# Score items in pairs, key scores together, two heads in one transposing DMA, packed steps reordered

## The chip, the cores and the metric

One core of a Trainium2 chip runs the whole kernel. The metric is the device time of one execution in microseconds. In the profile PE is the matrix engine (TensorE) and PEld its weight loads, DVE is VectorE, ACT is ScalarE, POOL is GpSimd, and SP issues the DMAs.

## The reference, cut to what matters

Three stages run behind each other for 8 batches of 576 tokens.

```
# 1 packed attention, 8 heads of 64, 32 packed rows p per head
p_packed = softmax(p k^T / 8) v              # "key scores" s, then a, pp
out      = softmax(q p_packed^T / 8) p_packed # "second scores", a2
# 2 gated MLP on x = out (576 x 512)
u, v   = split(gelu(x @ w_in));  v_n = layernorm(v) * g_ln
v_s    = w_sg @ v_n + b_sg;      x = x + (u * v_s) @ w_out
# 3 four causal attention experts of width 64, top 2 of 4 per token
for e in range(4):
    a   = softmax(causal((x wq_e)(x wk_e)^T / 8))
    out += weight_e * (a (x wv_e)) wo_e
```

## The kernel before, in words

The kernel goes through the batches in a software pipeline. A turn of the loop consists of `front(b)` and `back(b)`. `front` forms the v half of the gated MLP (`v_tiles`) and its u half (`u_tile`, four tiles). `back` forms v_s (`vs_tile`, four tiles), then the q and k products of the experts (`qk`, groups 0 to 3; the first part from gh, the second from a2 and bdq), their values and gate logits (`vlog`, token groups VT[0] to VT[2]) and the gates. The weights w_out are folded into the expert weights, and the packed rows of the next batch are folded into w_in, w_qk and w_vg (`wprime`, `bdw`: blocks wp, bdq, bdv).

The experts' attention is cut into ten items i = (j, pr): j is a group of 128 query tokens (j = 4 has 64), and pr is a pair of experts (0 for even i, 1 for odd i). S_i are the scores with their softmax (`att`: a product with 64 rows for each of the two experts; `att_last` for j = 4, S8 and S9, with a full-height padded copy `last_q`). T_i transposes the weights `at` into PSUM (block aTp), and ACT copies them out (aT). y_j multiplies with the values, ACT copies the result and DVE forms its remainder; o_j multiplies with w_o and ACT copies the result to ot. The last items of a batch run in the turn of the next one, and go(names) issues them.

The packed attention of the next batch runs in steps between the qk and vlog products of `back`. Q is one of two groups of four heads: K and Q join the planes of k and q on POOL (kT, qT), s is the key score with its exponential a, a (step) transposes it (a1T, DVE copies to a1t), p is the product with v (pp), P transposes that (ppT), r the second scores. Before that, SP turns k and q by a DMA (`turn`: DMA transpose; `keep`: write to DRAM; `planes`: read back). The list TURN holds those steps, and tick() issues the next of them.

PE and SP follow the program order (manual_schedule). The order on DVE, ACT and POOL is set by a scheduler. All PSUM blocks share one ring, pd, of four buffers, and each block of PE's work takes the next one.

In one batch turn of before, the row-split score items S1, S3, S5, S4 and S6 stand singly between the vs tiles and behind them, and S7, S0, S2 between qk and wp products. Key scores s0 and s1 are apart, with the exponential of one over other products.

Of the kernel before, what the change touches and what calls it, by code (L numbers as in the profile page):

```python
# [7 lines left out]
F32 = mybir.dt.float32  # L8
# [3 lines left out]
U16 = mybir.dt.uint16  # L12
# [5 lines left out]
P = 128  # L18
# [8 lines left out]
def packed_attention_mlp_moe_kernel(  # L27
# [18 lines left out]
    nc = tc.nc  # L46
    B, H, S, D = q.shape
# [10 lines left out]
    sb = ctx.enter_context(tc.tile_pool(name="sb", bufs=1))  # L58
# [1 line left out]
    psum = ctx.enter_context(tc.tile_pool(name="psum", bufs=1, space=bass.MemoryType.PSUM))  # L60
    dram = ctx.enter_context(tc.tile_pool(name="dram", bufs=1, space=bass.MemoryType.DRAM))

    NB = {"A": 4, "B": 10, "C": 4, "D": 12, "a": 3, "p": 1, "T": 4, "nat": 2, "x": 2, "t": 4, "v2": 1, "y": 1, "W": 2}
    NPS = 4
    BY = {"A": 1152, "B": 576, "C": 640, "D": 576, "a": 1152, "p": 576, "T": 512, "t": 576, "W": 2048}

    def slot(tag, dt=F32, w=None, name=None):
        t = sb.tile([P, BY[tag]], dt, tag=tag, name=name or ("s" + tag), bufs=NB[tag])
        return t if w is None else t[:, :w]
# [8 lines left out]
    def dap(src, offset, ap):  # L78
        return bass.AP(tensor=src.tensor, offset=src.offset + offset, ap=ap)
# [87 lines left out]
    def load_w_sg(c):  # L167
        if c < 4:
            if c % 2 == 0:
                wst["t"] = slot("A", name="wst")  # L170
            wst[c] = wst["t"][:, (c % 2) * S:(c % 2) * S + S]
        else:
            wst[c] = slot("p", name="wst")
        nc.sync.dma_start(wst[c][:TOK[c]], moe_w_sg[c * P:c * P + TOK[c], :])


# [148 lines left out]
    def load_nat(name, src, b, j):  # L325
        if (b, name) == (0, "q"):
            t = slot("T", w=512, name=name)
        elif (b, name) == (0, "v"):
            if j % 2 == 0:
                NAT["v2"] = slot("A", name=name)  # L330
            t = NAT["v2"][:, (j % 2) * 512:(j % 2) * 512 + 512]
        elif (b, name) == (0, "k") and j >= 2:
            t = slot("D", w=512, name=name)
        else:
            t = nat_slot(F32, name)
        t = t.rearrange("p (h n) -> p h n", h=2)
        off = (b * H + 2 * j) * S * D
        NAT[name, b, j] = t
        if b:
            for h in range(2):  # L340
                nc.sync.dma_start(t[:, h].rearrange("p (c d) -> p c d", c=4),
                                  dap(src, off + h * S * D, [[D, P], [P * D, 4], [1, D]]))
            if j % 2 == 0:
                r = small.tile([P, 2, D], F32, tag="rem", name=name + "r", bufs=2)
                for h in range(2):
                    nc.sync.dma_start(r[:, h], dap(src, off + (512 + 32 * h) * D, [[S * D, 4], [D, 32], [1, D]]))
                NAT[name + "r", b, j // 2] = r.rearrange("p h d -> p (h d)")
            return
        nc.sync.dma_start(t, dap(src, off, [[4 * D, P], [S * D, 2], [1, 4 * D]]))
        if j % 2 == 0:  # L350
            if name == "v":
                r = small.tile([P, 2 * D], F32, tag="rem", name=name + "r", bufs=2)
            else:
                if "rem" not in NAT:
                    NAT["rem"] = sb.tile([P, 512], F32, tag="y", name="rem", bufs=NB["y"])
                i = 2 * "kq".index(name) + j // 2
                r = NAT["rem"][:, i * P:(i + 1) * P]
            nc.sync.dma_start(r, dap(src, off + 512 * D, [[S * D, 4], [2 * D, 32], [1, 2 * D]]))
            NAT[name + "r", b, j // 2] = r
# [6 lines left out]
    def tick(n=1):  # L366
        for _ in range(min(n, len(TURN))):
            for f in TURN.pop(0):
                f()

    def p1_steps(b):
# [12 lines left out]
        def load(name, src, j):  # L384
            load_nat(name, src, b, j)
# [6 lines left out]
            act_copy(pT, pt[:, :2 * P], scale=0.125)  # L392
            s["pT"] = pT

        def turn(name, src, h):
            x = sb.tile([P, S], U16, tag="x", name=name + "x", bufs=NB["x"])
            nc.sync.dma_start_transpose(x, src[b, h].bitcast(U16))
            if h % 2 == 0:
                s[name + "x", h // 2] = dram.tile([P, 2, S], U16, name=f"turned_{name}{b}{h}")
            s["x", name, h] = x  # L400

        def keep(name, h):
            nc.sync.dma_start(s[name + "x", h // 2][:, h % 2, :], s.pop(("x", name, h)))
# [154 lines left out]

        last = None
        for name, src in (("k", k), ("q", q)):  # L560
            for h in range(H):
                TURN.append([lambda a=last: a and keep(*a), lambda a=(name, src, h): turn(*a)])
                last = (name, h)
        TURN.append([lambda a=last: keep(*a)])

        def f_():
            for j in range(4):
                planes("k", j)
            for j in range(2):
# [148 lines left out]
    def u_tile(b, m):  # L718
        s = ST[b]
        u = slot("D", name="u")  # L720
        pt = pd("u")
        n = 0
        for x, y in PASSES:
            for Q in range(2):
                for h in range(2):
                    nc.tensor.matmul(pt[:, h, :HALF], wp_part(b, 0, y, Q)[:, m * P:(m + 1) * P],  # L726
                                     s["a2", Q][x][:, hs(h)], start=n == 0, stop=n == 5)
                n += 1
        nc.scalar.activation(two(u), pt[:, :, :HALF], AF.Gelu_apprx_tanh)
        s["u", m] = u  # L730
# [308 lines left out]
    def front(b, go):  # L1039

        for cs in VT:
            v_tiles(b, cs)
            tick(2)
        u_tile(b, 0)
        go("T0")
        tick()
        for m in range(1, 4):
            u_tile(b, m)
            tick()

    def back(b, go):
        def do_all(names):

            for n in names.split():
                if (b + 1, n) in STEP:
                    STEP.pop((b + 1, n))()
                elif n[0] in "STyo":
                    go(n)

        if b:  # L1060
            go("S1")
            vs_tile(b, 0)
            go("S3")
            vs_tile(b, 1)
            go("T1 y0 T2 S5")
            vs_tile(b, 2)
            go("T3 o0 S4 y1")
            vs_tile(b, 3)
        tick(len(TURN))
        if b + 1 < B:  # L1070
            STEP.pop((b + 1, "f"))()
        go("T5 S6 o1 T4")
        bdw(b)
        weights(b + 1, ("in1", "in0"))
        nxt = attention(b)
        qk_mm(b, 0)
        go("S7 y2")
        qk_out(b, 0)
        do_all("K0 S8 T6 o2 s0 S9 T7")
        keep_last_q(b, 0)  # L1080
        qk(b, 2)
        if b + 1 == B:
            go("y3 T8 o3")
            vlog(b, VT[2])
            go("T9")
            vlog(b, VT[0])
            go("y4")
        else:
            do_all("y3 a0 K1 s1 Q0 p0 T8 o3 a1 T9 Q1")
            vlog(b, VT[2])  # L1090
            do_all("y4 p1 P0 o4 P1 r0 r1")
            if b + 2 < B:
                ahead(b + 2)
            vlog(b, VT[0])
            tick()
# [12 lines left out]
        tick()
        if b + 1 < B:
            wp_mm(b + 1, 1)  # L1110
        qk_gated(b, 3, False)
        tick()
        if b + 1 == B:
            qk_out(b, 3)
            return nxt
        wp_out(b + 1, 1)
        qk_out(b, 3)
        wprime(b + 1, 0)
        weights(b + 1, ("qk", "vg"))
# [144 lines left out]
```

## Time and profile before

| | |
|---|---|
| median of three runs | 879.46 us (879.15 to 879.69) |
| profiled execution, its own time | 878.9 us |
| its span | 877.0 us |
| mean granted clock of TensorE | 0.981 |
| PE busy | 825.4 us (94%) |
| DVE busy | 583.3 us (67%) |
| ACT busy | 424.7 us (48%) |
| POOL busy | 188.4 us (21%) |

The span is the time from the first to the last instruction of the profiled execution; the time of the execution is 1.9 us more. Busy times are sums over all instructions of an engine, and engines run beside one another.

### The profile page before, as it was taken

Reading aid. Unit: us, or ns where it says so; the run is one execution under the profiler, and the core shown is the slowest. Engines: PE = TensorE matmul, PEld = TensorE weight load, DVE = VectorE, ACT = ScalarE, POOL = GpSimd, SP = SyncE. Lnnn points to the kernel's source line nnn. Section 1 sums busy time; section 2 is a strip of 40 time slices with the busy share of each in tenths; the row PEclk is TensorE's granted clock in tenths of the full one; section 3 lists DMA queues with packets and bytes.
Section 4 is the critical chain, followed back from the end, with each engine's and each line's share of the span. In section 5 each row is a group of like instructions: output and inputs, shape, how many; then the busy total and the mean of one; then the engine's idle time right before and its main releaser. Section 6 shows DMA issues by size and latency. Waiting matters only on the chain.

```text
span 877.0 us, 19165 instructions
## 1 busy us (share of the span) xinstructions
PE 825.4 (94%) x7517; PEld 697.9 (80%) x7517; DVE 583.3 (67%) x1387; ACT 424.7 (48%) x973; POOL 188.4 (21%) x272
## 2 busy tenths in 40 slices
PE   4687988999999999999999999999999999999987
PEld 2356877788888888888789888888789888888965
DVE  6766644876577674877477665867488566866265
ACT  2356332565436542655346552655346543745245
POOL 0002051312332151303322141404222141300000
PEclk9798889999999999999999999999999999999989
DMA  9886673537445563548245563549263660100001
GB/s 307 229 208 176 143 234 86 146 88 224 114 99 143 140 188 86 154 109 231 76 130 116 148 188 83 154 111 237 69 153 89 171 178 7 74 13 26 19 1 55
DMA packets 178725, 114.08 MB, mean 130 GB/s; under 512 B 118282, under 2 KB 166666, under 8 KB 175820
## 3 DMA queue, kind: packets, MB, share of 16 engines
q1 hardware_dynamic: 178636, 112.87, 48.0%
q8 instruction: 59, 0.97, 0.5%
q14 instruction: 30, 0.25, 0.1%
HBM read 68.26 MB, written 29.63 MB: 112 GB/s over the span
## 4 chain that ended last, share of the span: by engine, by line
PE 75%; DVE 5%; ACT 2%; issue 1%; POOL 0%; ACTq 0%; DVEq 0%; POOLq 0%
PE vs L744 10%; PE qk L789 10%; PE y L968 6%; PE vlog L832 6%; PE qk L801 5%; PE v L676 5%; PE o L999 5%; PE sc L885 4%; PE u L726 4%; PE aTp L939 4%; PE vlog L836 3%; PE sc L915 2%; PE wp L625 1%; PE aTp L953 1%; PE s L448 1%
## 5 line engine op out<-in xcount | busy, mean ns | idle before, releaser
L744 PE MATMUL vs<-w_sg,vnh 128*128 128x288 f32 x512 | 92.8, 304 | 0.7 <-DVE w_sg L85 0.7
L789 PE MATMUL qk<-gh,w_qk 128*128 128x288 f32 x512 | 92.7, 304 | 0.0
L789 PEld LDWEIGHTS qk<-gh,w_qk 128*128 128x128 f32 x512 | 76.2, 193 | 10.6 <-issue 7.1
L82 ACT ACTIVATE aT<-aTp 128x512 f32<-128x512 f32 (+4 forms) x160 | 60.9, 434 | 44.1 <-PE aTp L939 36.2
L744 PEld LDWEIGHTS vs<-w_sg,vnh 128*128 128x128 f32 x512 | 75.7, 191 | 5.3 <-issue 3.0
L416 POOL COPY kT<-kp 128x576 uint16<-128x576 uint16 x56 | 48.0, 921 | 147.4 <-DMA kp<-turned_k 98.1
L898 ACT ACTIVATE at<-sc,nm 128x256 f32<-128x256 f32 (+3 forms) x128 | 66.3, 524 | 26.7 <-DVE nm L889 21.1
L691 POOL TENSOR_TENSOR rstd<-rstd,mhalf 128x1 f32<-128x1 f32 x40 | 36.4, 917 | 152.8 <-DVE rstd L690 152.8
L968 PE MATMUL y<-aT,v 128*64 128x128 f32 (+2 forms) x960 | 61.6, 267 | 0.2 <-ACT aT L82 0.2
L902 DVE TENSOR_SCALAR at<-at,sm,gw 128x256 f32<-128x256 f32 (+3 forms) x128 | 60.1, 511 | 2.3
L832 PE MATMUL vlog<-w_vg,gh 128*128 128x260 f32 (+1 forms) x320 | 60.8, 287 | 0.0
L968 PEld LDWEIGHTS y<-aT,v 128*64 128x64 f32 (+1 forms) x960 | 48.4, 140 | 14.1 <-issue 7.6
L819 POOL CAST last_q<-qk 64x64 fp32r<-64x64 f32 x64 | 14.9, 233 | 196.6 <-ACT qk L809 103.1
L789 PE MATMUL qk<-gl,w_qk 128*128 128x288 f32 x256 | 55.6, 299 | 0.0
L744 PE MATMUL vs<-w_sg,vnl 128*128 128x288 f32 x256 | 55.3, 298 | 0.0
L889 DVE TENSOR_REDUCE nm<-sc 128x2 f32<-128x256 f32 (+3 forms) x64 | 52.6, 822 | 1.7
L999 PE MATMUL o<-w_o,y 128*128 128x512 f32 x192 | 52.5, 408 | 0.5 <-ACT y L978 0.5
L832 PEld LDWEIGHTS vlog<-w_vg,gh 128*128 128x128 f32 (+1 forms) x320 | 47.4, 178 | 3.5 <-issue 2.8
L885 PE MATMUL sc<-qk 64*128 64x256 f32 (+3 forms) x384 | 47.4, 352 | 0.0
L416 POOL COPY qT<-qp 128x576 uint16<-128x576 uint16 x56 | 44.6, 870 | 11.0 <-DMA qp<-turned_q 11.0
L939 PE MATMUL aTp<-ident,at 128*128 128x128 f32 x320 | 46.6, 277 | 0.0
L899 DVE TENSOR_SCALAR sm<-sm 128x2 f32<-128x2 f32 x64 | 16.4, 256 | 44.9 <-ACT at L898 44.5
(208 smaller groups left out, 1927.9 us busy)
## 6 DMA issues: line engine op xcount, KB each, us to landing
w_in<-kept_in SPq DMA_DIRECT2D x14, 1024.0 KB
w_qk<-kept_qk SPq DMA_DIRECT2D x8, 1024.0 KB
out_dram<-ot SPq DMA_DIRECT2D x32, 256.0 KB
turned_k<-kx SPq DMA_DIRECT2D x56, 144.0 KB
turned_q<-qx SPq DMA_DIRECT2D x56, 144.0 KB
kp<-turned_k SPq DMA_DIRECT2D x56, 144.0 KB
qp<-turned_q SPq DMA_DIRECT2D x56, 144.0 KB
v<-in_v_dram SPq DMA_DIRECT2D x56, 128.0 KB
```

Of the source, the lines that this page charges most:

```text
L82: nc.scalar.activation(o, i, AF.Copy, scale=scale)
L416: nc.gpsimd.tensor_copy(w[:, i], t[:, i].rearrange("p h n -> p (h n)"))
L744: nc.tensor.matmul(pt[:, h, :HALF], s["vn", c][x][:, cols], w_sg[y][:, c, hs(h)], start=(c, x, y) == (0, 0, 0), stop=False)
L789: nc.tensor.matmul(o[:, h, :], W["w_qk"][y][:, m, cols], s["g", m][x][:, hs(h)], start=first and (m, x, y) == (0, 0, 0), stop=not first an ...
L832: nc.tensor.matmul(pt[:n, ci, :260], s["g", m][x][:, c * P:c * P + n], W["w_vg"][y][:, m, :], start=(m, x, y) == (0, 0, 0), stop=False)
L885: nc.tensor.matmul(pt[:, e, :L], qs[x][r, j * P:L], ks[y][r, :L], start=i == 0, stop=i == 2)
L889: nc.vector.tensor_reduce(nm, pt[:, :, :L], axis=AX.X, op=OP.max, negate=True)
L898: nc.scalar.activation(ats[e][:, :L], pt[:, e, :L], AF.Exp, bias=nm[:, e:e + 1], accum_out=sm[:, e:e + 1])
L902: nc.vector.tensor_scalar(ats[e][:, :L], ats[e][:, :L], sm[:, e:e + 1], s["w"][:, j, 2 * pr + e:2 * pr + e + 1], op0=OP.mult, op1=OP.mult)
L939: nc.tensor.transpose(pt[:, e, c * P:c * P + P], ats[e][:, c * P:c * P + P], ident)
L968: nc.tensor.matmul(pt[64 * e:64 * e + 64, pr * w:pr * w + w], s["v2"][:m, c, col:col + D], s["aT", pr, e, j][c][:m, :], start=c == 0, stop ...
L999: nc.tensor.matmul(pt, ys[:, pr, x, :], W["w_o"][y][:, pr, :], start=i == 0, stop=i == 5)
```

## The change: what it does

It concerns the order of PE's and SP's program and the shape of two DMAs. Score items are issued two behind each other (S1 S3 and S0 S2 of one expert pair each, S5 S4 and S6 S7 of both), S1 S3 ahead of the last u tile; S8 and S9 are adjacent as well. The key scores s0 s1, and then a0 a1, stand together behind K0 and K1; the second scores r0 and r1 are separate with P1 between them, and wp_mm follows r1. The vlog order is VT[1], VT[2], VT[0]. y2 follows o1, ahead of bdw. The DMA transposes take two heads at once (9 steps in TURN in place of 17), and tick() is called less often in the front. v's rest is loaded by `load_rest` behind the two heads of its load.

```diff
-    NB = {"A": 4, ..., "a": 3, "p": 1, "T": 4, "nat": 2, "x": 2, "t": 4, ...}
+    NB = {"A": 4, ..., "a": 3, "p": 2, "T": 4, "nat": 2, "t": 4, ...}
...
-        def turn(name, src, h):
-            x = sb.tile([P, S], U16, tag="x", name=name + "x", bufs=NB["x"])
-            nc.sync.dma_start_transpose(x, src[b, h].bitcast(U16))
...
+        def turn(name, src, j):
+            x = sb.tile([P, 2, S], U16, tag="p", name=name + "x", bufs=NB["p"])
+            rows = src[b, 2 * j:2 * j + 2].rearrange("h s d -> (h s) d").bitcast(U16)
+            nc.sync.dma_start_transpose(x.rearrange("p h s -> p (h s)"), rows)
...
         for cs in VT:
             v_tiles(b, cs)
-            tick(2)
+            tick()
         u_tile(b, 0)
         go("T0")
-        tick()
         for m in range(1, 4):
             u_tile(b, m)
+            if m == 2:
+                go("S1 S3")
             tick()
...
-            go("S1")
             vs_tile(b, 0)
-            go("S3")
+            go("T1 T2 y0 S5 S4")
             vs_tile(b, 1)
-            go("T1 y0 T2 S5")
+            go("o0 T3")
             vs_tile(b, 2)
-            go("T3 o0 S4 y1")
+            go("y1 T5 T4 S6 S7")
             vs_tile(b, 3)
...
-        go("T5 S6 o1 T4")
+        go("o1 y2")
         bdw(b)
...
-        qk_mm(b, 0)
-        go("S7 y2")
-        qk_out(b, 0)
-        do_all("K0 S8 T6 o2 s0 S9 T7")
+        qk(b, 0)
+        do_all("T6 o2 T7 K0 S8 S9 K1")
         keep_last_q(b, 0)
         qk(b, 2)
...
-            do_all("y3 a0 K1 s1 Q0 p0 T8 o3 a1 T9 Q1")
-            vlog(b, VT[2])
-            do_all("y4 p1 P0 o4 P1 r0 r1")
...
+        do_all("y3 s0 s1 T8 T9 o3 a0 a1 y4 p0 Q0 Q1 o4 P0")
         vlog(b, VT[1])
+        do_all("p1 r0 P1")
+        vlog(b, VT[2])
+        do_all("r1")
+        if b + 1 < B:
+            wp_mm(b + 1, 1)
...
-        nxt("S0" if b + 1 < B else "S8")
...
-        nxt("S2" if b + 1 < B else "S6")
...
+        nxt("S0 S2" if b + 1 < B else "S8 S6")
```

What this does to the order on the engines is shown at three places of the turn from batch 3 to batch 4. First PE around the key scores, in before from y3 on. s_5395 is the key score of the second group of heads; that of the first, s_5262, stands 22 rows earlier, with a score item, a transpose, a qk group and y3 between.

```order
L968 MATMUL y<-aT,v_4128 64x128 x16
L475 MATMUL a1T<-ident,a_5273 128x128 x4
L448 MATMUL s_5395<-kT,pT 32x288 x8
L490 MATMUL pp<-v,a1t 32x64 x16
L496 MATMUL pp<-vr,a1r 32x64 x8
L953 MATMUL aTp<-ident,at 128x128 x4
L953 MATMUL aTp<-ident,at 64x128
```

The same place in after, from y3 to y4 (the last row).

```order
L970 MATMUL y<-aT,v_4093 64x128 x16
L449 MATMUL s_5276<-kT,pT 32x288 x8
L449 MATMUL s_5292<-kT,pT 32x288 x8
L955 MATMUL aTp<-ident,at 128x128 x4
L955 MATMUL aTp<-ident,at 64x128
L955 MATMUL aTp<-ident,at 128x128 x4
L955 MATMUL aTp<-ident,at 64x128
...
L476 MATMUL a1T<-ident,a_5287 128x128 x4
L476 MATMUL a1T<-ident,a_5303 128x128 x4
L970 MATMUL y<-aT,v_4093 64x64 x20
```

Both key scores, both last transposes (T8 T9), o3 and both a1T now stand in one run, and y4 follows them; in before pp followed a1T with only eight products between.

Second, ACT at the same place in after; a_5287 and a_5303 are the exponentials of the two key scores, the aT copies are those of T8 and T9, and the last y is y4's.

```order
L980 ACTIVATE y<-y 128x256
L458 ACTIVATE a_5287,st_5285<-s_5276,st_5285 128x576
L458 ACTIVATE a_5303,st_5301<-s_5292,st_5301 128x576
L82 ACTIVATE aT<-aTp 128x512
L82 ACTIVATE aT<-aTp 64x128
L82 ACTIVATE aT<-aTp 128x512
L82 ACTIVATE aT<-aTp 64x128
L82 ACTIVATE ot<-o 128x512
L980 ACTIVATE y<-y 128x2x64
```

In before the exponential of s_5262 stands five rows of ACT's list ahead of that of s_5395, and T8's copies are behind the second; now both exponentials come ahead of all four aT copies.

Third, the front. PE in after, from the third u tile to the first vs products; the two sc rows are S1 and S3.

```order
L728 MATMUL u<-a2h,wph 128x288 x4
L728 MATMUL u<-a2h,wpl 128x288 x4
L728 MATMUL u<-a2l,wph 128x288 x4
L887 MATMUL sc<-qk 128x128 x6
L887 MATMUL sc<-qk 128x256 x6
L728 MATMUL u<-a2h,wph 128x288 x4
L728 MATMUL u<-a2h,wpl 128x288 x4
L728 MATMUL u<-a2l,wph 128x288 x4
L746 MATMUL vs<-w_sg_114,vnh 128x288 x2
```

In before S1 stood behind the last u row and S3 behind the first vs tile; now both stand ahead of the last u tile.

ACT in the front of after: the u copies are the gelus of the third and fourth u tile, then come a load of ACT's function table, the exponentials of S1 and S3 (two each) and the aT copies of T1.

```order
L731 ACTIVATE u<-u 128x576
L699 ACTIVATE vnh<-vg,rstd 128x512
L706 ACTIVATE vnl<-vg,rstd 64x512
L731 ACTIVATE u<-u 128x576
L900 ACT_TABLE_LOAD
L900 ACTIVATE at,sm_6007<-sc,nm_6005 128x128 x2
L900 ACTIVATE at,sm_6025<-sc,nm_6023 128x256 x2
L82 ACTIVATE aT<-aTp 128x128 x2
```

In before vnh and vnl stood behind the last gelu, and between S1's and S3's exponentials there was one copy (gh) of the first vs tile.

## Rows read from the trace of the kernel before

**Rows 1.** Stretches: length, busy (instructions) of each engine, granted clock, DMA share, GB/s.

```profile
112.96:206.61 93.65, 86.42 (x764) 73.34 (x763) 60.09 (x137) 42.33 (x91) 27.17 (x38) 0.96 0.51 136
...
498.44:595.72 97.28, 96.59 (x920) 82.85 (x919) 66.90 (x160) 49.31 (x114) 26.76 (x37) 1.00 0.54 140
...
790.60:877.00 86.40, 78.41 (x681) 66.39 (x680) 43.13 (x118) 39.06 (x106) 1.85 (x8) 0.96 0.07 25
```

**Rows 2.** Waits of PE, 206 to 790 us: total, times, longest.

```profile
PE pp L490 <- DVE a1t L477: 2.5, 6, 0.6
PE s L448 <- ACT ppT L509: 1.9, 6, 0.3
```

**Rows 3.** Timeline of PE at score items: start, length, instruction, tiling, shape, count.

```profile
504.97 0.97 PE L885 MATMUL sc<-qk 64*128 64x512 f32 x6
505.87 1.53 PE L968 MATMUL y<-aT,v 128*64 128x128 f32 x24
...
573.19 0.43 PE L749 MATMUL vs<-w_sg,vnl 66*128 66x288 f32 x2
573.54 0.62 PE L885 MATMUL sc<-qk 64*128 64x256 f32 x6
574.09 0.79 PE L744 MATMUL vs<-w_sg,vnh 128*128 128x288 f32 x4
574.73 0.43 PE L744 MATMUL vs<-w_sg,vnl 128*128 128x288 f32 x2
574.99 0.69 PE L744 MATMUL vs<-w_sg,vnh 128*128 128x288 f32 x4
575.51 0.43 PE L744 MATMUL vs<-w_sg,vnl 128*128 128x288 f32 x2
```

**Rows 4.** Timeline of PE behind the key scores of the second group.

```profile
521.61 0.65 PE L490 MATMUL pp<-v,a1t 128*32 128x64 f32 x32 [0.37 <-DVE a1t L477]
...
523.07 1.63 PE L999 MATMUL o<-w_o,y 128*128 128x512 f32 x6
524.54 0.60 PE L475 MATMUL a1T<-ident,a 128*128 128x128 f32 x4
524.97 0.71 PE L953 MATMUL aTp<-ident,at 128*128 128x128 f32 x5
525.44 0.48 PE L832 MATMUL vlog<-w_vg,gh 128*64 128x260 f32 x2
```

**Rows 5.** Timelines of ACT and of DVE at the key scores.

```profile
522.31 0.74 ACT L457 ACTIVATE a<-s,st 128x576 f32<-128x576 f32 x1 [1.81 <-DVE st L455]
...
523.35 0.75 ACT L82 ACTIVATE aT<-aTp 128x512 f32<-128x512 f32 x2 [0.21 <-PE aTp L953]
...
521.47 0.74 DVE L455 TENSOR_REDUCE st<-s 128x1 f32<-128x576 f32 x1
```

**Rows 6.** Timelines of ACT, DVE and PE from the table load to T1.

```profile
571.36 1.28 ACT L898 ACT_TABLE_LOAD   x1 [0.23 <-DVE nm L889]
...
573.90 0.60 DVE L902 TENSOR_SCALAR at<-at,sm,gw 128x128 f32<-128x128 f32 x2
...
577.91 0.38 PE L939 MATMUL aTp<-ident,at 128*128 128x128 f32 x2
```

**Rows 7.** Waits of PE in the turn of batch 0.

```profile
PE s L448 <- POOL kT L416: 3.1, 2, 2.3
PE pp L490 <- DMA v<-in_v_dram: 1.5, 2, 1.0
PE a1T L475 <- ACT a L457: 1.2, 1, 1.2
PE ppT L507 <- DVE pp L501: 0.7, 1, 0.7
```

**Rows 8.** Longest wait of PE in the last turn.

```profile
PE aTp L953 <- DVE sm L899: 2.4, 1, 2.4
```

**Rows 9.** Stretches that show the granted clock, columns as in the first group.

```profile
129.70:136.00 6.30, 4.92 (x90) 3.97 (x89) 2.63 (x9) 1.48 (x3) 3.69 (x5) 1.00 0.17 44
846.50:853.30 6.80, 6.35 (x56) 5.09 (x57) 3.74 (x12) 2.17 (x7) 0.00 (x0) 0.50 0.01 2
```

More of the change, by code (lines that the diff above doesn't have):

```diff
@@ L61, in packed_attention_mlp_moe_kernel @@
     dram = ctx.enter_context(tc.tile_pool(name="dram", bufs=1, space=bass.MemoryType.DRAM))
-    NB = {"A": 4, "B": 10, "C": 4, "D": 12, "a": 3, "p": 1, "T": 4, "nat": 2, "x": 2, "t": 4, "v2": 1, "y": 1, "W": 2}
+    NB = {"A": 4, "B": 10, "C": 4, "D": 12, "a": 3, "p": 2, "T": 4, "nat": 2, "t": 4, "v2": 1, "y": 1, "W": 2}
     NPS = 4
@@ L172, in load_w_sg @@
         else:
-            wst[c] = slot("p", name="wst")
+            wst[c] = slot("D", name="wst")
         nc.sync.dma_start(wst[c][:TOK[c]], moe_w_sg[c * P:c * P + TOK[c], :])
@@ L342, in load_nat @@
                                   dap(src, off + h * S * D, [[D, P], [P * D, 4], [1, D]]))
[L343 to L347, printed above, removed]
             return
@@ L359, in load_nat, with load_rest @@
             NAT[name + "r", b, j // 2] = r
+    def load_rest(b, Q):
+        r = small.tile([P, 2, D], F32, tag="rem", name="vr", bufs=2)
+        for h in range(2):
+            nc.sync.dma_start(r[:, h], dap(v, ((b * H + 4 * Q) * S + 512 + 32 * h) * D, [[S * D, 4], [D, 32], [1, D]]))
+        NAT["vr", b, Q] = r.rearrange("p h d -> p (h d)")
     ST = {}
@@ L393, in make_pT, with keep @@
             s["pT"] = pT
-        def turn(name, src, h):
-            x = sb.tile([P, S], U16, tag="x", name=name + "x", bufs=NB["x"])
-            nc.sync.dma_start_transpose(x, src[b, h].bitcast(U16))
[L398 to L403, printed above, removed]
+        def turn(name, src, j):
+            x = sb.tile([P, 2, S], U16, tag="p", name=name + "x", bufs=NB["p"])
+            rows = src[b, 2 * j:2 * j + 2].rearrange("h s d -> (h s) d").bitcast(U16)
+            nc.sync.dma_start_transpose(x.rearrange("p h s -> p (h s)"), rows)
+            s["x", name, j] = x
+        def keep(name, j):
+            s[name + "x", j] = dram.tile([P, 2, S], U16, name=f"turned_{name}{b}{j}")
+            nc.sync.dma_start(s[name + "x", j], s.pop(("x", name, j)))
         def planes(name, j):
@@ L560, in p1_steps @@
         for name, src in (("k", k), ("q", q)):
-            for h in range(H):
-                TURN.append([lambda a=last: a and keep(*a), lambda a=(name, src, h): turn(*a)])
-                last = (name, h)
+            for j in range(4):
+                TURN.append([lambda a=last: a and keep(*a), lambda a=(name, src, j): turn(*a)])
+                last = (name, j)
         TURN.append([lambda a=last: keep(*a)])
@@ L570, in f_ @@
                 load("v", v, j)
+                load_rest(b, j)
         STEP[b, "f"] = f_
@@ L1075, in back @@
         nxt = attention(b)
-        qk_mm(b, 0)
-        go("S7 y2")
-        qk_out(b, 0)
-        do_all("K0 S8 T6 o2 s0 S9 T7")
+        qk(b, 0)
+        do_all("T6 o2 T7 K0 S8 S9 K1")
         keep_last_q(b, 0)
         qk(b, 2)
-        if b + 1 == B:
-            go("y3 T8 o3")
-            vlog(b, VT[2])
[L1085 to L1088, printed above, removed]
-            do_all("y3 a0 K1 s1 Q0 p0 T8 o3 a1 T9 Q1")
-            vlog(b, VT[2])
-            do_all("y4 p1 P0 o4 P1 r0 r1")
[L1092 to L1095, printed above, removed]
-        vlog(b, VT[1])
+        do_all("y3 s0 s1 T8 T9 o3 a0 a1 y4 p0 Q0 Q1 o4 P0")
+        vlog(b, VT[1])
+        do_all("p1 r0 P1")
[3 more added lines that the diff above has]
+            wp_mm(b + 1, 1)
+        if b + 2 < B:
+            ahead(b + 2)
+        vlog(b, VT[0])
         tick()
         gates(b)
-        if b + 1 == B:
-            go("o4")
         qk(b, 1)
@@ L1103, in back @@
         tick()
-        nxt("S0" if b + 1 < B else "S8")
+        qk_packed(b, 3, True)
         tick()
-        qk_packed(b, 3, True)
-        nxt("S2" if b + 1 < B else "S6")
-        tick()
-        if b + 1 < B:
-            wp_mm(b + 1, 1)
+        nxt("S0 S2" if b + 1 < B else "S8 S6")
         qk_gated(b, 3, False)
```

## The prediction

> **What bounds the kernel now.** I read the page's engine line first (it is in the table above): PE is busy 825.4 of 877.0 us, DVE, the next, 583.3. Shares over the whole span can mislead, so I then cut the span at the start of each batch's bdq products and read engine times stretch by stretch [rows 1]. Three kinds of stretch appear: six steady turns of about 97.3 us, PE busy about 96.6 in each at full granted clock; the turn of batch 0 (93.65 long, 86.42 busy, clock 0.96); and the last turn with the tail (86.40 long, 78.41 busy, 0.96). Third, the waits of PE over the six steady turns: two groups, a1T's copy by DVE ahead of pp and ppT's copy by ACT ahead of the second scores, six times each [rows 2]. I take 0.37 us for the first, the idle time at its row of 521.61 [rows 4], and 1.9 / 6 = 0.32 for the second: 0.69 a turn. No steady wait is on a DMA. So in six of eight turns time can be won only by fewer or cheaper PE instructions or from these 0.69 us, and any new wait of PE is paid in full.
>
> **Fourth view: what a visit to another tiling costs.** The change leaves the number of matmuls as it is. It alters how often PE goes from full 128-row products to products split by rows (scores at 64 rows, key scores and wp at 64*32) and back. Pitches, starts against starts, price this [rows 3]: a score item of 256 columns starts at 573.54 and its successor at 574.09, so 0.55; one of 512 takes 504.97 to 505.87, 0.90. The slope is 0.35 for 256 columns, so 0.20 of each visit is not columns. The neighbours pay too: the two products ahead of the visit take 573.19 to 573.54, 0.35, where two like them take 574.73 to 574.99, 0.26; the four behind it 0.64 (574.09 to 574.73) against 0.52 (574.99 to 575.51). Together 0.20 + 0.09 + 0.12 = 0.41, called 0.4: 0.2 for each change of tiling.
>
> **The change, part by part.**
>
> *Score items in pairs.* Of ten items a turn, eight are split by rows and stand alone in before; in after they are S1 S3, S5 S4, S6 S7 and S0 S2: four visits fewer, 1.6 us. S8 and S9 use the full-height padded last_q, so their standing together saves no visit.
>
> *Key and second scores, wp.* In before the 64*32 visits of a turn are bdq/bdv, s0, s1, the two second scores together, wp, wp: six. In after they are bdq/bdv, s0 s1, second scores of Q=0, second scores of Q=1 with wp behind them, wp: five. One fewer, 0.4. Sum of both parts: −2.0 a steady turn. Bounds: 0, if the drain is paid between any two score blocks, and 2.5, if each wp or s block also sheds its own entry too.
>
> A rule speaks against part of this. The row shows transposes whose last output is 64 wide (the aTp group at 524.97) followed by vlog at 128*64 with no idle time and at 0.47 start to start for five transposes [rows 4]. The Trainium skill, "TensorEngine Tiling (Array Packing)", section "Key Properties", says that changing the tiling mode, not just the tile, drains the TensorE. Counted by nominal modes on that rule, a steady turn of before has 44 changes and one of after 37, seven fewer and not ten, which would make this term −1.4.
>
> *The two old waits.* pp now stands behind a1T, a1T and y4 (20 products), so a1T's copy is hidden; ppT's copy gets vlog or pp over it. −0.7 a turn, with 0.1 coming back where ppT of Q=1 follows its pp after only eight products of second scores.
>
> *New wait at the key scores.* In before, s0 and s1 are far apart. In after, ACT's order is y3, both exponentials, four aT copies, ot. Let Z be the start of s0. I take y3's copy and DVE's remainder to end at Z+1.0. From the durations then [rows 5]: DVE's reduction of s0 (0.74) at Z+1.75; its exponential (0.74, then its sum) at Z+2.6; DVE's small operations on s0, which wait for it, stand ahead of the reduction of s1, so this ends at Z+3.8 and its exponential at Z+4.65; then two aT copies of T8 (0.75) and two of T9 end near Z+6.1. PE meanwhile has s0 s1 (an estimate of 1.5), the transposes of T8 and T9 (0.47 each), o3 (523.07 to 524.54, 1.5), two a1T (0.43 each) and is at y4 by Z+4.9 [rows 4]. y4 needs T9's copies: a new wait of about 1.3 us. Bounds: 0, if DVE's small operations don't hold the second reduction up, and 2 if the o3 copy or a PSUM buffer is late as well.
>
> *New wait in the front.* S1 and S3 now stand ahead of the last u product, and T1 T2 directly behind the first vs tile; in before vs1 lay over them. T1 started at 577.91; without vs1 (574.09 to 577.91, 3.8) and with one visit less it comes at about 573.75 [rows 3, 6]. Its data: in before ACT loads its table from 571.36 to 572.65, runs the exponentials, and DVE's scaling ends at 574.5. In after the last gelu comes ahead of the same load, and S3's operations come between; I take 574.8. New wait: about 1.1. Bounds: 0 (the load moves up with the earlier reductions) and 2.4 (S3's exponentials ahead of the scaling of S1).
>
> So new waits come to 1.3 + 1.1 + 0.1 = 2.5; y0, which in before follows T1 with only its own two copies between, loses about 0.3 now that T2 stands between: net +2.2. A steady turn: −2.0 − 0.7 + 2.2 = −0.5; six of them −3.0.
>
> *Turn of batch 0.* Six changes of tiling fewer, −1.2. Its waits are 3.1 on POOL's kT joins, 1.5 on v's DMA, 1.2 on an exponential and 0.7 on pp's scaling: 6.5 [rows 7]. In after s0 stands behind qk of group 2, which covers most of the joins (I take 1.3 of the 3.1 to be left, since POOL starts them as before behind the first last_q cast); v has arrived by then; the second a1T waits about 1.2 and ppT 0.7, as before; 3.2 left, −3.3. But in the front of batch 1 ACT's order in after has the exponentials of S1 ahead of the last gelu, with two more table loads of 1.28 (19 in the program against 17); one fits in an idle stretch, the other adds to the 1.1 of the other turns: +2.4. Net −2.1. Bounds: −6 (no slow stretch and no front wait) and +1.
>
> *Tail.* Five changes fewer, −1.0; o4 now directly behind y4, +0.75 for y4's copy and remainder; +0.5 for S9 and qk's remainder. The 2.4 wait of T9 on its normalisation [rows 8] stays. Net +0.25.
>
> *At nothing:* the nine steps of two-head transposing DMAs instead of 17, v's rest loaded later, the slots: no steady wait is on a DMA or POOL [rows 2], and POOL, the joins' engine, is busy 26.76 of 97.28 [rows 1]: the work of a whole turn lies over them. Without that cover late kT joins would cost what they cost batch 0, 3.1 in two waits [rows 7].
>
> **Sum.** −3.0 − 2.1 + 0.25 = −4.9. The profiled execution took 878.9 (span 877.0); so 874.0, and as the median of before lies 0.56 above its profiled execution, **874.6** as a median. A measurement of this kernel tells about 0.2% (1.8 us) from no change.
>
> **Rivals.**
> 1. *The new waits don't appear* (scheduler order runs ahead of my chain: DVE's small operations wait less, the table load comes early). Six times 2.5 and some 2.4 in batch 0 are saved: 874.6 − 17.4 = 857. For it: ACT is busy only 49.3 of 97.3. Against: both chains are made of measured durations in a fixed order. Chance 0.15.
> 2. *The other side: the granted clock falls behind the new waits.* In before the clock is at 0.50 over 846.5 to 853.3, just behind the 2.4 wait; but it holds 1.00 over 129.7 to 136.0, with the 1.2 wait in it [rows 8, 9]. Half clock for 3.4 us costs 1.7. My new waits are 1.1 to 1.3, near the harmless one. A fall in each of seven turns is +12: 886. It decides from the fourth fall on (−4.9 + 4 × 1.7 = 1.9). Chance 0.15.
> 3. *Only nominal mode changes count* (three savings fewer in each steady turn, two in the tail, 0.2 each): +4.0, so 878.6. The clean passage of the transposes [rows 4] speaks against it. Chance 0.13.
> 4. *The merging saves nothing:* each score block pays its own entry, from its own weights or its PSUM buffer. The waits remain: 874.6 + 14 = 889. Against: products of one shape pay nothing extra behind each other in before, 0.52 for four [rows 3]. Chance 0.05.
>
> **How the numbers follow.** Forecast 0.52, its own range 867 to 880 (two terms of ±0.5 a turn and batch 0's bounds). Holding 8 in 10: 858 leaves out half of rival 1, 883 half of rival 2 and rival 4. Faster than 877.7: most of the forecast (0.46), all of rival 1, under half of rival 3: 0.66. Within 0.2%: 0.14. Slower than 881.2: rivals 2 and 4: 0.20.
>
> **What would show it.** Stretches between bdq's starts near 96.8 instead of 97.3, with PE busy near 94.5; paired score items of 12 products whose second half costs columns only (S0 S2: 0.20 + 0.175 + 0.35 instead of 0.48 + 0.55, and cheaper neighbours); PE waits per steady turn of about 1.3 on ACT's aT ahead of y4 and of about 1.1 on DVE's scaled at ahead of T1; no wait of pp on a1T. Batch 0's stretch should be near 91.5, the tail's near 86.6. The prediction is wrong if PE busy falls by less than 1.5 a turn (merging), if the waits total 0.5 or 4 (chains), or if the granted clock of a steady stretch is below 1.00.

## The result, and the profile after

The changed kernel takes 887.8 us (median of four runs, 887.67 to 891.6) against 879.58 for the kernel before, beside which it ran: a ratio of 1.0103 with an interval of 1.0075 to 1.013. It is slower, clear of the 0.2% that can be told from no change. The forecast was 874.6 with a range of 858 to 883, so the time lies outside it and on the other side. The profiled execution took 887.67, span 886.0, which is 9.0 more than before.

First the page's engine line of the kernel after: PE has become hardly less busy in sum (825.4 before), so its shares tell nothing.

```profile
PE 823.7 (93%) x7517; PEld 705.5 (80%) x7517; DVE 578.0 (65%) x1387; ACT 428.0 (48%) x975; POOL 185.9 (21%) x272
```

Then its stretches, cut at the bdq products as in [rows 1], with the startup ahead of them.

```profile
0.00:117.64 117.64, 82.15 (x567) 61.38 (x567) 78.06 (x180) 47.78 (x99) 6.27 (x17) 0.88 0.76 214
117.64:212.61 94.97, 89.20 (x794) 77.08 (x793) 63.00 (x146) 48.07 (x103) 28.72 (x40) 0.93 0.46 128
212.61:311.41 98.80, 96.60 (x920) 84.02 (x918) 66.75 (x161) 49.41 (x113) 25.11 (x36) 0.98 0.54 136
...
508.94:607.81 98.87, 96.65 (x921) 84.25 (x919) 66.17 (x160) 49.39 (x113) 24.94 (x35) 0.98 0.51 135
...
706.79:804.15 97.36, 95.16 (x921) 82.94 (x919) 66.58 (x161) 49.31 (x113) 23.26 (x33) 1.00 0.27 78
804.15:886.00 81.85, 74.08 (x652) 63.29 (x650) 38.91 (x108) 35.68 (x95) 1.87 (x8) 0.98 0.08 27
```

Against before the startup is 4.7 longer (it ended at 112.96), batch 0's stretch 1.3, five steady turns about 1.5 each and the sixth 0.05, and the tail is 4.5 shorter: 4.7 + 1.3 + 7.5 − 4.5 = 9.0. Two things stand out. The one steady turn at granted clock 1.00 (the undisturbed turn below) is as long as before; the five at 0.98 are 1.4 to 1.6 longer than that one, 7.4 together. And the largest growth of a single stretch is in the startup, which the prediction had not priced.

Third, the waits of PE in one steady turn of the kernel after (they answer to [rows 2], whose two are gone).

```profile
PE aTp L941 <- ACT at L900: 1.7, 1, 1.7
PE a1T L476 <- ACT a L458: 0.3, 1, 0.3
PE o L1001 <- ACT a L458: 0.2, 1, 0.2
```

The first is T1's, and around it stand these rows of PE (start, length; idle time ahead and its releaser in brackets).

```profile
581.20 0.42 PE L751 MATMUL vs<-w_sg,vnl 66*128 66x288 f32 x2
583.32 0.93 PE L941 MATMUL aTp<-ident,at 128*128 128x128 f32 x6 [1.70 <-ACT at L900]
584.18 0.66 PE L970 MATMUL y<-aT,v 128*64 128x128 f32 x8
584.77 2.01 PE L887 MATMUL sc<-qk 64*128 64x384 f32 x12
```

DVE in the same front, some 6 us earlier, and in the last row at the scaling that T1 needs:

```profile
576.81 0.43 DVE L888 TENSOR_TENSOR sc<-sc,causal 128x256 f32<-128x256 f32 x1
577.15 0.16 DVE L692 TENSOR_SCALAR rstd<-mv 128x1 f32<-128x1 f32 x1
...
582.83 0.60 DVE L904 TENSOR_SCALAR at<-at,sm,gw 128x128 f32<-128x128 f32 x2
```

And ACT behind it, up to the table load:

```profile
578.40 0.72 ACT L699 ACTIVATE vnh<-vg,rstd 128x512 fp32r<-128x512 f32 x1 [1.78 <-POOL rstd L693]
579.03 0.71 ACT L706 ACTIVATE vnl<-vg,rstd 64x512 fp32r<-64x512 f32 x1
579.64 0.63 ACT L731 ACTIVATE u<-u 128x576 f32<-128x576 f32 x1
580.29 1.28 ACT L900 ACT_TABLE_LOAD   x1
```

The reader is to see a queue: S1's mask (576.81) stands on DVE ahead of rstd of the last v tile, POOL and ACT's vnh wait for it until 578.40, the last gelu waits behind vnh and vnl although its products have long ended, and the table load waits behind that gelu. The prediction named DVE's scaling as what T1 waits for, the profile names ACT: the first of the two scalings ends at 583.18 and the sum of S3's last exponential at 583.30, so both ends of the same late chain come within 0.2 us of each other. Then the clock: three of the one-microsecond stretches behind this wait.

```profile
585.00:586.00 1.00, 1.00 (x10) 1.00 (x10) 0.89 (x3) 0.90 (x4) 0.00 (x0) 0.56 0.00 0
586.00:587.00 1.00, 1.00 (x7) 0.56 (x4) 1.00 (x3) 0.00 (x0) 0.00 (x0) 0.50 0.06 16
...
588.00:589.00 1.00, 1.00 (x8) 1.00 (x7) 0.97 (x2) 0.90 (x5) 0.00 (x0) 0.73 0.00 0
```

A mean of 0.56 is 0.88 us at half, one of 0.73 is 0.54 us. So the granted clock falls to its half level (1.2 of 2.4 GHz) at about 585.1, 1.8 us after PE had started again, and is back at about 588.5, 3.4 us later.

### The profile page after: what moved, and what is told of

Same layout as the page of the kernel before. It is cut to its first block, busy times and chain, and to the rows that moved or that the text cites. A ratio compares the mean times of both kernels' runs of the same rounds, so it can differ in the third digit from the quotient of the medians.

```text
span 886.0 us, 19144 instructions
## 1 busy us (share of the span) xinstructions
PE 823.7 (93%) x7517; PEld 705.5 (80%) x7517; DVE 578.0 (65%) x1387; ACT 428.0 (48%) x975; POOL 185.9 (21%) x272
## 4 chain that ended last, share of the span: by engine, by line
PE 64%; DMA 13%; DVE 9%; ACT 7%; SPq 3%; issue 2%; POOL 1%; ACTq 0%; POOLq 0%
PE vs L746 10%; PE qk L791 9%; PE vlog L834 7%; PE y L970 5%; PE o L1001 4%; PE qk L803 4%; PE sc L887 4%; PE aTp L941 4%; PE vlog L838 3%; DMA w_in<-kept_in 3%; DMA qp<-turned_q 3%; DMA qx<-in_q_dram 3%; DMA raw_in<-in_moe_w_in_dram 2%; DVE bnst L688 2%; DVE vg L694 2%
## 5 line engine op out<-in xcount | busy, mean ns | idle before, releaser
L746 PE MATMUL vs<-w_sg,vnh 128*128 128x288 f32 x512 | 95.1, 310 | 0.7 <-DVE w_sg L85 0.7
L791 PE MATMUL qk<-gh,w_qk 128*128 128x288 f32 x512 | 90.6, 299 | 0.0
L746 PEld LDWEIGHTS vs<-w_sg,vnh 128*128 128x128 f32 x512 | 78.6, 198 | 6.4 <-issue 2.6
L82 ACT ACTIVATE aT<-aTp 128x512 f32<-128x512 f32 (+4 forms) x160 | 59.1, 435 | 12.5 <-PE aTp L941 10.8
L970 PE MATMUL y<-aT,v 128*64 128x128 f32 (+2 forms) x960 | 57.8, 264 | 0.8 <-ACT aT L82 0.8
L904 DVE TENSOR_SCALAR at<-at,sm,gw 128x256 f32<-128x256 f32 (+3 forms) x128 | 55.2, 473 | 1.8
L970 PEld LDWEIGHTS y<-aT,v 128*64 128x64 f32 (+1 forms) x960 | 46.6, 137 | 12.2 <-issue 5.7
L840 ACT ACTIVATE v<-vlog 128x512 f32<-128x512 f32 (+1 forms) x24 | 12.6, 525 | 81.9 <-PE vlog L838 81.9
L941 PEld LDWEIGHTS aTp<-ident,at 128*128 128x128 f32 x320 | 37.9, 144 | 16.2 <-ACT at L900 11.4
L417 POOL COPY qT<-qp 128x576 uint16<-128x576 uint16 x56 | 42.6, 834 | 38.4 <-DMA qp<-turned_q 38.3
```

The source lines that it names most:

```text
L82: nc.scalar.activation(o, i, AF.Copy, scale=scale)
L417: nc.gpsimd.tensor_copy(w[:, i], t[:, i].rearrange("p h n -> p (h n)"))
L746: nc.tensor.matmul(pt[:, h, :HALF], s["vn", c][x][:, cols], w_sg[y][:, c, hs(h)], start=(c, x, y) == (0, 0, 0), stop=False)
L791: nc.tensor.matmul(o[:, h, :], W["w_qk"][y][:, m, cols], s["g", m][x][:, hs(h)], start=first and (m, x, y) == (0, 0, 0), stop=not first an ...
L904: nc.vector.tensor_scalar(ats[e][:, :L], ats[e][:, :L], sm[:, e:e + 1], s["w"][:, j, 2 * pr + e:2 * pr + e + 1], op0=OP.mult, op1=OP.mult)
L941: nc.tensor.transpose(pt[:, e, c * P:c * P + P], ats[e][:, c * P:c * P + P], ident)
```

## The experiments

My theory after the result: the early place of T1 makes a wait, the wait makes the clock fall, and the startup has a cause of its own. Rivals: the place of S1 S3 counts rather than T1's; the clock falls because of what stands there; the DMAs crowd the startup.

**e1: T1 later.** The changed kernel with this edit.

```diff
             vs_tile(b, 0)
-            go("T1 T2 y0 S5 S4")
             vs_tile(b, 1)
-            go("o0 T3")
+            go("T1 T2 y0 S5 S4")
             vs_tile(b, 2)
-            go("y1 T5 T4 S6 S7")
+            go("o0 T3 y1 T5 T4 S6 S7")
             vs_tile(b, 3)
```

> The changed kernel, but T1 T2 y0 S5 S4 stand behind the second vs tile and o0 T3 y1 T5 T4 S6 S7 behind the third. Theory A (T1 comes too early for its scaled scores, PE waits 1.7 us in each of six fronts, and behind five of these waits the granted clock is at half for some 3 us, which costs about 1.4): all of it goes, steady stretches of 95.7, in all 887.7 - 6 x 1.7 - 5 x 1.4 = 870.5. Theory B (the clock falls for another reason, the wait alone goes): steady stretches of 97.1 with the clock at 0.98, 877.5. Theory C (the late link is ACT's chain, and another block waits in T1's place): above 882.

Measured: 875.99, a ratio of 0.996 to before (0.9941 to 0.998). A steady stretch:

```profile
502.08:598.43 96.35, 95.37 (x920) 83.01 (x919) 65.98 (x160) 49.36 (x113) 24.87 (x35) 1.00 0.51 137
```

The first of its waits:

```profile
PE y L970 <- ACT aT L82: 0.4, 1, 0.4
```

T1's wait and all falls of the clock in steady turns are gone, as theory A has it. The time is still 5.5 above its 870.5. In each steady turn 0.65 of the gain is missing, since my edit put y1 directly behind T3, whose copies y1 now waits for (start to start, y1 to the next block takes 1.90 where it took 1.02 in the undisturbed turn); and the tail is 2.7 longer than in the changed kernel (84.52), for the reason given under *Tail* below.

**e2: S1 S3 behind the last u tile**, T1 left where the change put it.

```diff
             u_tile(b, m)
-            if m == 2:
+            if m == 3:
                 go("S1 S3")
```

> The changed kernel, but S1 S3 stand behind the last u tile, not ahead of it; T1 stays directly behind the first vs tile. Theory A (T1's early place makes the wait, but DVE's masks and reductions of S1 and S3 also delay the layer norm of the last v tile, and with it the last gelu and the table load): the wait shrinks from 1.7 to about 0.6, no fall of the clock, 874. Rival (the place of S1 S3 is without effect, only T1's counts): wait 1.7 and clock as in the changed kernel, 887.

Measured: 870.52 (0.9892, 0.9869 to 0.9915). Batch 0's stretch and a steady one:

```profile
117.45:208.56 91.11, 86.38 (x793) 74.84 (x792) 63.07 (x146) 45.33 (x101) 28.87 (x40) 0.96 0.48 133
498.05:594.53 96.48, 94.86 (x920) 82.89 (x918) 66.11 (x160) 49.34 (x113) 24.91 (x35) 1.00 0.51 138
```

T1's wait in the second of these stretches:

```profile
PE aTp L941 <- DVE at L904: 1.1, 1, 1.1
```

T1's wait shrinks to 1.1 (1.5 in batch 0's stretch), no clock falls behind it in any of the seven turns, and batch 0's stretch loses 3.9 us. So both places matter: that of S1 S3 makes the layer norm and the gelu late, that of T1 leaves no room for it.

**e6: one line on the startup.** The kernel before, with the slot of the fifth tile of w_sg as in the change. The same line is part of the changed kernel.

```diff
         else:
-            wst[c] = slot("p", name="wst")
+            wst[c] = slot("D", name="wst")
```

> The kernel before with one line of the change: the fifth tile of w_sg is loaded into a slot of D, not of p. The orders of DVE and ACT in the startup are then those of the changed kernel. Theory A (this reordering makes the startup 4.7 us longer): first bdq product at about 117.6 instead of 113.0, 884.3 in all, later stretches as before. Rival (the two-head transposing DMAs crowd the startup's loads): startup as before, 879.6.

Measured: 883.58 (1.0039, 1.0018 to 1.0059), 4.1 over the median of before. Its startup:

```profile
0.00:116.55 116.55, 81.96 (x567) 60.75 (x567) 77.41 (x179) 47.42 (x99) 6.26 (x17) 0.91 0.76 213
```

The startup grew by 3.6, with the order on PE unchanged. It is not the only stretch that moved: three steady turns are 0.6 to 0.9 longer, batch 0's is 0.8 longer and the tail 2.3 shorter, so theory A's "later stretches as before" did not hold. Where in the startup: PE's rows of the fold products, first in before, then in e6.

```profile
63.30 3.70 PE L300 MATMUL fold<-fqk,woT 128*128 128x512 f32 x8 [2.04 <-ACT woT L82]
...
64.64 6.76 PE L300 MATMUL fold<-fqk,woT 128*128 128x512 f32 x8 [3.67 <-ACT woT L82]
```

And the same products in the kernel after.

```profile
66.17 5.40 PE L300 MATMUL fold<-fqk,woT 128*128 128x512 f32 x8 [3.66 <-ACT woT L82]
```

The slot moves the scheduler's list, in e6 as in the kernel after: on ACT the copies to w_qk and woT now stand behind both pairs of a2h, not between them, and on DVE the 1.2 us of wpl stand directly ahead of the transposes that a2h waits for. The wait is 1.6 longer (3.67 for 2.04), and the clock is at half behind it: the eight products take 6.76 in e6 and 5.40 in the kernel after, for 3.70.

**e5: the reverse**, the changed kernel with that line undone (slot("p")).

> The changed kernel with the fifth tile of w_sg in p again, no more. Theory A (that line alone makes most of the longer startup): startup near 114, 884. Rival (the startup is longer because of the DMAs): 117.6, 887.7. The steady stretches stay at 98.8.

Measured: 884.51 (1.0066, 1.0042 to 1.0089); startup 114.20, 3.4 less than in the kernel after. Five of six steady turns again have the long form (98.8 to 98.9), but the short one is another one:

```profile
505.75:603.11 97.36, 95.15 (x921) 82.94 (x919) 66.10 (x160) 49.26 (x113) 25.04 (x35) 1.00 0.50 137
603.11:702.01 98.90, 96.70 (x921) 83.98 (x919) 65.55 (x160) 49.58 (x113) 25.07 (x36) 0.98 0.51 136
```

**e7: e1 and e5 together.**

> The changed kernel with T1 behind the second vs tile and the fifth tile of w_sg in p again. Theory A for both: 870.5 - 4.7 = 865.8. If only T1's place counts: 870.5. If only the slot counts: 883.

Measured: 874.78 (0.9949, 0.9933 to 0.9964), startup 115.27, steady turns 96.3. Only 1.2 below e1 in the median and 9 above theory A's 865.8; the startup is 2.0 shorter than e1's. The fold wait is back at 2.04, but the clock fell behind it here, as it did not in before, and the eight products again take 5.40 for 3.70: that 1.7 stayed.

**e10: the DMAs alone.** The kernel before with `turn`, `keep`, the nine steps and `load_rest` of the change.

> The kernel before with the two-head transposing DMAs, the nine steps and the later load of v's rest alone, and the fifth tile of w_sg in p as before; the order on PE, DVE and ACT is that of before. Theory A (these DMAs are hidden): 879.5, startup 113, steady stretches 97.3. Rival (they crowd the loads of the startup, some 2 us of the 4.7 that it grew by): startup 115, 881.5.

Measured: 877.03 (0.9974, 0.9957 to 0.9992). Startup, batch 0's stretch and a steady one:

```profile
0.00:113.36 113.36, 81.03 (x567) 60.85 (x567) 77.99 (x180) 47.68 (x99) 6.27 (x17) 0.91 0.77 215
113.36:205.63 92.27, 86.29 (x763) 73.34 (x763) 60.18 (x137) 42.25 (x91) 29.80 (x41) 0.96 0.55 143
497.50:594.84 97.34, 96.65 (x920) 82.86 (x919) 66.84 (x160) 49.42 (x114) 25.89 (x36) 1.00 0.55 138
```

Hidden in steady turns, no load on the startup (113.36 for 112.96), and, where no gain was expected, 1.4 gained in batch 0's stretch, where the wait of pp for v's DMA falls from 1.5 to 0.3.

**e12: one pair taken apart**, in e2 (so its neighbour for comparison is e2's 96.48).

```diff
+        nxt("S0" if b + 1 < B else "S8")
         qk_packed(b, 3, True)
         tick()
-        nxt("S0 S2" if b + 1 < B else "S8 S6")
+        nxt("S2" if b + 1 < B else "S6")
```

> e2_S1S3_behind_u with one pair taken apart again: S0 ahead of qk's packed part, S2 behind it, as before the change. Theory A (a visit to the row-split tiling costs 0.41): each steady stretch 0.4 longer, 96.9 for 96.5. Rival (a visit costs what the score block shows alone, 0.2 or less): 96.5 to 96.7.

Measured: one run, 874.35; its six steady stretches are 96.79 to 96.91, on average 0.32 more than e2's (0.20 to 0.42, turn by turn). One of them:

```profile
499.63:596.46 96.83, 95.22 (x920) 82.93 (x919) 67.17 (x160) 49.52 (x113) 25.14 (x36) 1.00 0.50 136
```

One more visit to the row-split tiling costs 0.32 here, nearer theory A than its rival. The other merged visits were not taken apart one by one.

**e8: both places and the slot.** S1 S3 as in e2, T1 as in e1 but with "T3 o0 y1 T5 T4 S6 S7" behind the third vs tile, the slot as before.

> The changed kernel with three edits: S1 S3 behind the last u tile, T1 T2 y0 S5 S4 behind the second vs tile with T3 o0 y1 behind the third, and the fifth tile of w_sg in p. Theory A (with both places right no wait is left in the front): steady stretches of 95.1 (96.5 of e2_S1S3_behind_u less its wait of 1.3), batch 0's stretch near 90, startup near 113 to 115; in all about 862. Rival (the wait moves on to T3 or y1 as in e1_late_T1, where y1 waited 0.9): stretches of 96, 867.

Measured: 857.61 (0.9755, 0.9734 to 0.9776), 4 below the expectation. A steady stretch and the tail:

```profile
490.28:585.39 95.11, 94.59 (x920) 82.81 (x919) 66.08 (x160) 49.58 (x113) 25.12 (x35) 1.00 0.50 138
775.76:857.30 81.54, 74.08 (x652) 63.28 (x650) 38.88 (x108) 35.68 (x95) 1.85 (x8) 0.98 0.08 27
```

**e9 and e13: the key scores.** e8 with the steps reordered; what e8 has, then e9's, then e13's.

```diff
-        do_all("y3 s0 s1 T8 T9 o3 a0 a1 y4 p0 Q0 Q1 o4 P0")
+        do_all("y3 T8 T9 s0 s1 o3 y4 a0 a1 o4 p0 Q0 Q1 P0")   # e9
+        do_all("y3 T8 T9 s0 s1 o3 a0 y4 a1 p0 Q0 Q1 o4 P0")   # e13
```

> As e8_both_places, and the steps around the key scores in another order: y3 T8 T9 s0 s1 o3 y4 a0 a1 o4 p0. Theory A (the two exponentials that stand ahead of T9's copies hold PE up in small pieces, about 0.8 a turn, of which the waits show 0.46): the pieces go, 0.8 a turn less than e8_both_places, 5 to 6 in all. Rival (a1T's copy and y4's remainder are late in their turn, as a1T's copy was in the kernel before): 0.4 a turn or less is left of it, 2 in all.

Measured: 862.88 (0.9823, 0.9795 to 0.985), 5 slower than e8, where both theories had it faster. PE no longer waits for the exponentials at o3 and a1T, but ppT now stands directly behind its pp, and there PE waits for DVE, a link that neither theory named. The steady turns are 95.26 to 97.02 long, 3.3 more than e8's in sum, and the tail is 3.3 longer (84.82); batch 0's stretch is 3.9 shorter. A steady stretch:

```profile
487.64:582.90 95.26, 94.33 (x920) 82.76 (x918) 65.95 (x160) 49.60 (x113) 24.89 (x35) 1.00 0.52 139
```

The only wait of PE in that stretch:

```profile
PE ppT L508 <- DVE pp L502: 0.9, 1, 0.9
```

> As e8_both_places, with the steps around the key scores as y3 T8 T9 s0 s1 o3 a0 y4 a1 p0 Q0 Q1 o4 P0: the aT copies ahead of both exponentials, y4 over the copy of the first a1T, o4 over that of pp. Theory A (the 0.9 a turn that e9_key_scores_later took out of the pieces stays out, and its new wait of 0.9 for pp's scaling is covered again): steady stretches of 94.2, 5 to 6 less than e8_both_places, near 852. Rival (one of the covers is too short): 94.8 or more, 856 or more.

Measured: 856.05 (0.973, 0.9702 to 0.9758), 2.7% under before and the lowest median of all, though only 1.6 below e8's, and the runs of the two overlap. A steady stretch and the tail:

```profile
486.90:581.21 94.31, 94.26 (x921) 82.90 (x919) 66.58 (x161) 49.71 (x113) 23.67 (x34) 1.00 0.55 140
769.98:854.50 84.52, 75.47 (x652) 64.68 (x650) 38.96 (x108) 35.80 (x95) 1.86 (x8) 0.95 0.08 26
```

The longest wait in the second, the tail:

```profile
PE aTp L955 <- DVE sm L901: 2.4, 1, 2.4
```

The steady turns have no wait left and are 0.80 shorter than e8's, as theory A has it (5 in six turns); the total is that of its rival all the same, since 3 of the gain are lost in the tail, where the 2.4 wait of [rows 8] is back.

**e11: a shorter wait.** The changed kernel with "T2 T1" for "T1 T2".

> The changed kernel with T2 ahead of T1, no more: PE's wait falls from 1.7 by T2's length of 0.35 to about 1.35. Theory A (the length of the wait decides whether the granted clock falls; waits of 1.25 in e2_S1S3_behind_u were followed by none, those of 1.7 in five of six turns): no or few falls, steady stretches near 97.0 at clock 1.00. Rival (the clock falls because of what stands at this place, whatever the wait): stretches near 98.4 at 0.98.

Measured: one run, 900.38. The swap does not decide between the theories, because it opened a second wait: y0 now stands directly behind T1. A steady stretch:

```profile
513.15:612.90 99.75, 96.88 (x920) 84.12 (x918) 66.45 (x160) 49.28 (x113) 24.87 (x35) 0.98 0.50 133
```

Its two longest waits of PE:

```profile
PE aTp L941 <- ACT at L900: 1.2, 1, 1.2
PE y L970 <- ACT aT L82: 1.1, 1, 1.1
```

With two waits of 1.2 and 1.1 close together the clock falls in all six turns.

**e14: the wait filled with work.** The changed kernel with this edit.

```diff
             vs_tile(b, 0)
+            fill = pd("fill")
+            for i in range(16):
+                nc.tensor.transpose(fill[:, 0, (i % 4) * P:(i % 4) * P + P], ident, ident)
             go("T1 T2 y0 S5 S4")
```

> The changed kernel with 16 transposes of the identity between the first vs tile and T1 (16 times 0.109 us, 1.74 in all, written to a PSUM block that nothing reads), so that PE works through the time in which it waited 1.7. Theory A (the idle time makes the granted clock fall, which costs 1.4 in five of six turns): the time to T1 stays, no fall, all steady stretches like the one undisturbed, 97.4 at clock 1.00, 880.5 in all. Rival (the clock falls because of what follows, T1 T2 y0 S5 S4 close together, and not because PE was idle): five or six stretches stay at 98.8 and 0.98, 887.7.

Measured: one run, 890.1 (before beside it 877.98). A steady stretch:

```profile
507.24:605.67 98.43, 97.31 (x936) 84.83 (x934) 66.41 (x160) 49.39 (x113) 25.53 (x36) 1.00 0.54 136
```

Its longest wait of PE:

```profile
PE y L970 <- ACT aT L82: 0.4, 1, 0.4
```

All six steady turns are at 1.00 with the same score items, T and y behind the filled place: PE's idle time, and not what follows, makes the clock fall here. In time the edit brought nothing. T1 starts as long after the vs tile as in the changed kernel, but from T1 to S5 PE now takes 2.50 for 1.45, since y0 waits for aT's copies and for DVE's reading of a vs block (0.4 and 0.2), so the turns are 98.4 long and not the 97.4 expected; and the startup (119.1) and the tail (85.7) came out longer.

## Why the prediction was wrong, step by step

Stretch by stretch the profile after is 9.0 longer where the sum had −4.9. The 13.9 between them are the startup (4.7), the steady turns (10.5, of which 7.4 are falls of the clock), batch 0's stretch (3.4) and the tail (−4.8).

**Startup: not in the sum, +4.7.** The step that failed is "At nothing: ... the slots". I asked only whether a steady wait is on a DMA or POOL, not whether a slot changes the lists that the scheduler writes for ACT and DVE in the startup. One line does that: e6 gives +3.6 from it alone, e5 takes 3.4 back. The other 1.1 to 1.3 of the startup are not settled; startups with the slot of before lie at 113.0 to 115.3, those with the slot of the change at 116.6 to 119.1.

**The wait in the front: right place, too small.** I wrote 1.1 (0 to 2.4) and it is 1.7 plus a restart. I counted S3's operations in, but not S1's mask ahead of rstd and the last gelu behind vnh; e2 shows that part by taking it away (1.1 is what then remains).

**The clock: the rival, not the forecast, in five of six turns.** I set the waits "near the harmless one" by comparing 1.1 to 1.3 with the 1.2 of batch 0. The wait was 1.7, the five falls make 7.4 us, and e14 shows the link. With a wait of 1.1, as in e2, there is no fall. But the wait that I compared with is not harmless as such: in the changed kernel its counterpart of 1.3, at 134.25 and now with waits of 0.8 and 0.3 just ahead of it, has the clock at half from 134.6 to 141.4, while behind the same three waits in e9, e11 and e14 there is no fall. Rival 2, with the deciding point at four falls, ended at 886 in its extreme, near the measured 887.8, but part of that agreement is the startup's.

**The merging: right, a little smaller.** Worked out 0.41 a visit, measured 0.32 (e12, one pair): −1.6 a steady turn if the other four are alike, not −2.0. The nominal-mode rival gets no support from the undisturbed turn: five visits at 0.32 (−1.6), the old waits gone (−0.7) and y0 shorter (−0.4: 0.58 for 0.97 start to start) against T1's wait with its restart (+1.9: 2.12 for 0.26 start to start) and the key scores (+0.8) give 0.0, and 0.05 was measured; three and a half visits would give +0.5.

**Key scores: right chain, wrong place, 0.8 for 1.3.** y4 began 5.84 after s0 where I had Z+6.1 for the copies, but without a wait of its own. PE came there later than I had it (Z+4.9), since o3 and a1T had to wait for the exponentials as well (0.16 and 0.31, more in pitch than shown as idle). e13 takes 0.80 out.

**Batch 0: −2.1 predicted, +1.3 measured.** The waits in the kernel after:

```profile
PE vs L749 <- DVE vnh L703: 2.5, 1, 2.5
PE a1T L476 <- ACT a L458: 1.6, 2, 1.3
PE s L449 <- POOL kT L417: 0.8, 1, 0.8
PE ppT L508 <- DVE pp L502: 0.7, 1, 0.7
```

The kT, a1T and ppT terms are within 0.5 of what I took. The two extra table loads do cost 2.5, but at the vs tile: behind S1's exponentials ACT loads the gelu's table back (182.90, 1.28 us), and the last gelu and the vnh that the vs products wait for come after it.

The clock is at half twice in this stretch, for 6.8 us each: from the waits around a1T on, and from 185.8, just ahead of the end of the vs wait (186.3); the mean is 0.93 for 0.96. In e2, which has no such loads, the stretch is 91.1, near my 91.5, though with one such fall in it.

**Tail: +0.25 predicted, −4.5 measured.** That the 2.4 wait of T9 "stays" was wrong: it is 0.2 here. DVE's rows in the kernel after:

```profile
857.88 0.58 DVE L926 TENSOR_SCALAR at<-at,sm,wl 128x576 f32<-128x576 f32 x1
858.41 0.43 DVE L888 TENSOR_TENSOR sc<-sc,causal 128x256 f32<-128x256 f32 x1
858.88 0.96 DVE L891 TENSOR_REDUCE nm<-sc 128x2 f32<-128x768 f32 x1
```

S9's scaling (the first row) now stands ahead of the next item's mask and reduction; in before it stood behind them:

```profile
845.36 0.96 DVE L889 TENSOR_REDUCE nm<-sc 128x2 f32<-128x768 f32 x1
846.23 0.57 DVE L924 TENSOR_SCALAR at<-at,sm,wl 128x576 f32<-128x576 f32 x1
```

In e1, e9 and e13 it is behind again (tails of 84.5 to 84.8), in e2 and e8 ahead (81.9 and 81.5), though no edit touches the tail's program. Up to 1.7 more is the clock, which is at half for 3.4 us of this tail where it was for 6.8 in before [rows 9]; in e6, with the order and the 2.4 wait of before and no fall behind it, the tail is 84.14 for 86.40. I had forecast neither, so the 4.5 are luck.

Taken together: without the clock and the slot the changed kernel would have been at about 887.8 − 7.4 − 3.4 = 877 (an estimate), inside the forecast's own range of 867 to 880, though by errors of both signs.

## What to carry to other kernels

On an engine that is nearly always busy, merging visits is worth its price only if no item comes to stand closer to its consumer than the chain on the other engines is long: count that chain with everything queued ahead of it on each engine, also work of other stages (a mask ahead of a layer norm, a gelu ahead of a table load). Any new wait should be priced twice, without and with a fall of the clock, and the version with more distance tried first: the same merging gave +1.0% here and −2.7% with its steps placed otherwise and the slot put back (e13). Where a scheduler writes some engines' orders, a slot or a step in one place can reorder another: compare those orders for the whole program, the startup and the end too.

## What the runs showed of the hardware that I had not expected

Behind a wait of 1.7 us in a stretch that is otherwise full, the granted clock went to half in five of six turns, 1.2 to 1.8 us after the wait's end and for 3.4 us; these turns are 1.4 to 1.6 longer than the sixth. Behind waits of 1.1, and of 1.5 once, it did not (e2). One turn in six is spared at the same wait (1.69), and it is not the same turn in two kernels (the sixth after batch 0 in the changed kernel, the fourth in e5), so I can't say what spares it. Nor does the length of a wait alone tell: the 2.04 of the startup was followed by a fall in e7, e8 and e13 and by none in before, e5, e9 and e10; the 2.4 of the tail came with one in before and with none in e6, the 2.5 at batch 0's vs tile with one in the changed kernel and with none in e14. And the idle time that the profile shows at a wait is less than the wait costs: around o3 it shows 0.16 and 0.31, and e13, where both are gone, is 0.80 a turn shorter.
